# Weight tiles of octets 6 and 7 of the second head group move to the end of the stream

## The chip, the cores and the metric

One core of one Trainium2 chip. The metric is the time of one execution on the device in microseconds (us), the median of several runs. The profile shows one execution of the program, with its span from the first instruction to the last.

## The reference, cut to what matters

Attention with a feature map gives x; a spectral mix over 64 modes and a product with `w_ch` follow.

```python
def phi(x):
    proj = np.einsum('bhsd,df->bhsf', x, w_phi)
    proj = proj - np.max(np.abs(proj), axis=-1, keepdims=True)
    return np.concatenate([np.exp(proj), np.exp(-proj)], axis=-1)
q_p, k_p = phi(q), phi(k)
kv = np.einsum('bhsf,bhsd->bhfd', k_p, v)
z = np.sum(k_p, axis=2)
x = einsum('bhsf,bhfd->bhsd', q_p, kv) / (einsum('bhsf,bhf->bhs', q_p, z)[..., None] + 1e-06)
# x is put together as (8 batches, 576 rows, 512 = 8 heads x 64)
X = np.fft.rfft(x, axis=1)[:, :64]
Y[:, :64] = X @ (w_r + 1j * w_i)      # for each mode m a 512 x 512 matrix
u = x + np.fft.irfft(Y, n=576, axis=1)
out = u + np.maximum(u @ w_ch, 0.0)
```

`q`, `k`, `v` are (8, 8, 576, 64), `w_r` and `w_i` (64, 512, 512), all float32: the two weights alone are 134 MB.

## The kernel before, in words

**Tiles and units.** The 512 channels are split into four head groups g = 0 to 3 (two heads, 128 channels), the batches into four pairs bp. Attention runs over 16 units (g, bp). The 64 modes are split into eight *octets* o. A *weight tile* holds, for one group of 128 input channels and one octet, either w_r or w_i (1 MB in bfloat16, cast on the way in): 4 x 8 x 2 = 64 tiles, keys (g, 2o + i), with i = 0 for w_r and 1 for w_i. Tiles are numbered here 1 to 64 in the order of the stream. The list `wq` (lines 359 to 365) is that order: all 16 tiles of groups 0 and 1, then 12 tiles (octets 0 to 5) each of groups 2 and 3, and last octets 6 and 7 of groups 2 and 3, eight tiles. POOL issues all loads of weights, `kb`, `qb` and most of `vn` on one queue, in program order. A tile has one of nine buffers (`pw`), and each `next_w` issues the next load once its buffer is free.

**Attention loop** (lines 514 to 588, steps n = -2 to 16). Each step works on several units at different stages, then `freq` and `keep_x` bring a finished unit's spectrum to `XTb[g % 2]`: two buffers, so group g + 2 writes over group g. When a group's last unit is through (n = 4, 8, 12, 16), its keys join `mixq`. `some` takes keys from it, eight or nine in step 4, three in a later one (one more in step 12), calls `mix` (line 473: eight matmuls of the tile with the spectrum, 0.66 us in all at full clock) and issues the next load. Sums over the groups go to `yacc`.

**End phase.** After the loop come the remaining tiles in `while mixq` (line 977). `left` is the number of tiles still in `mixq` after the one just mixed. When the last tile of an octet is mixed, the octet's result y is transposed and multiplied by `w_ch` to give z (the octet step), and `park` puts both aside. Between tiles, `fill` takes pieces from the list `todo`:

- `turn` and `hold(i)`: transposes of one of 36 chunks of 128 rows of x (`xT`, copied from PSUM by DVE) and its product with `w_ch`, copied to `xw` by ACT. The inverse DFT tables (`inverse_tables`) are made by DVE and ACT in steps, one for each `hold`. The last three chunks' products stay in PSUM (`Channels.hold`) and are ended by `only_x` and `only_w`.
- `Absorb.all` for the other 33 chunks: adds the inverse transform of octets 0 to 5 (or 0 to 6) to x and to xw. It needs `lay`, which spreads the parked octets over the batches of a pair by DVE (two transposes of about 0.6 us), and so octet 5. For each chunk DVE adds to x, and ACT copies to xw; every second one of the first 28 takes another way (`aside`), where ACT copies to `rl` and POOL adds to xw. `full` is their order; chunks of the `direct` pairs, which need octet 6 as well, come last.

How many pieces go behind a tile is computed from `left` (lines 996 to 1001). Behind the last mix only what octets 6 and 7 still add remains: `Pair` and the written-out order `plan` (line 640), the relu, the sum and the stores by SP.

**Order.** All engine calls go through `InOrder` (line 29), which keeps them in program order on their engine. The profile therefore gives line 37, that of the helper, for all of them, and groups are told by their tiles' names: `pt<-wt,XT` is a mix, `pt<-ident_b,xs` a `turn`, `pt<-wchb,xT` the product of a `hold`, `pt` or `pp<-yall,CI` and `<-zall,CI` an `Absorb`.

Of the kernel before, what the change touches and what calls it, by code (L numbers as in the profile page):

```python
# [43 lines left out]
def kernel(  # L44
# [311 lines left out]
        return wt  # L356

    wts = {}
    wq = [(g, mg) for g in range(2) for mg in range(2 * NO)]
    wq += [(g, mg) for g in (2, 3) for mg in range(12)]  # L360
    wq += [(g, 2 * o + i) for o in (6, 7) for g in (2, 3) for i in range(2)]
    order = list(wq)
    wq.remove((0, 5))
    wq.insert(1, (0, 5))
# [108 lines left out]
    def mix(g, w, wt, XT, bank):  # L473

        o, i = w // 2, w % 2
        late = g >= 2 and o >= 6
        first, last = i == 0 and not (late and g == 3), i == 1 and not (late and g == 2)
        if first:
            pys[o] = bank()
        py = pys[o]  # L480
        for r in range(2):
            for j in range(4):
                pe.matmul(
                    py[32 * j:32 * j + 32, :],
                    lhsT=XT[:, i, r, :, :, :, 4 * o + j].rearrange("p t x b -> p (t x b)"),
                    rhs=wt[:, j, r, :], start=(first and r == 0), stop=(last and r == 1),
                )
        if last and g == 0:
            act.copy(yacc[:, o, :], pys.pop(o))
        elif last and g < NG - 1:  # L490
            dve.tensor_tensor(
                out=yacc[:, o, :], in0=pys.pop(o), in1=yacc[:, o, :], op=ALU.add)
# [22 lines left out]
    for n in range(-2, len(units) + 1):  # L515
        P, Q, K, R = (unit(n + i) for i in (-1, 0, 1, 2))
        X = 0 if n < 4 else 6 if n == 4 else 3
        end = n == len(units)
        if Q:
            Q.exp_q(0)  # L520
        if K:
            K.rows_k(0)
            K.exp_k(0)
        if Q:
            Q.weigh_v2()
            if n + 3 == len(units):
                unit(n + 2).load_v_parts()
            elif unit(n + 2):
                unit(n + 2).load_v()
        if P:  # L530
            P.freq()
            assert not any(key[0] == P.g - 2 for key in mixq)
            P.keep_x()
            if P.bp == NP - 1:
                mixq += [key for key in order if key[0] == P.g and (P.g < 2 or key[1] < 12)]
        if Q:
            Q.cols_q(1)
            Q.exp_q(1)
        some(1 if X else 0)
        if K:  # L540
            K.rows_k(1)
            K.exp_k(1)
        if Q:
            Q.kv()
        some(2 if n == 4 else 0)
        if K:
            K.rows_q(0)
            K.rows_k(2)
            K.rows_q(2)
            K.rows_q(1)  # L550
        if Q:
            Q.cols_q(2)
            Q.keep_kv()
            Q.exp_q(2)
        if K:
            K.exp_k(2)
            K.weigh_v()
        some(1 if X and not end else 0)
        if R:
            R.turn_k(0)  # L560
        if K:
            K.shift_q()
        if R:
            R.turn_k(1)
        if Q:
            Q.num(0)
        if K:
            K.cols_q(0)
        if R and unit(n + 4):
            unit(n + 4).load_k()  # L570
        if Q:
            Q.num(6)
        if R:
            R.turn_q(0)
            R.turn_q(1)
            if unit(n + 4):
                unit(n + 4).load_q()
        if Q:
            Q.num(12)
        some(0 if end else X - 2 + (n == 12))  # L580
        if n == -1:
            forward_table()
        if n < 3:
            next_w((2, 3, 2, 3, 2)[n + 2])
        elif n == 3:
            next_w(1)
        if n == 6:
            pool.dma_start(wchb, moe_w_ch.rearrange("(dc p) e -> p dc e", p=128))
    assert not pys
    mixq += order[-8:]  # L590
    pm_cm.__exit__(None, None, None)
    pin_cm.__exit__(None, None, None)
    ps1_cm.__exit__(None, None, None)
# [121 lines left out]
    class Channels:  # L715
# [4 lines left out]
        def turn(self):  # L720
# [2 lines left out]
            for g in range(NG):  # L723
                pe.transpose(pt[:, g, :], x[:, g, :], ident_b)
            self.xT = pb.tile([128, 4, 128], BF16, name="xT")
            dve.tensor_copy(self.xT, pt)

        def product(self):
            pf = bank()
# [2 lines left out]
                          start=(g == 0), stop=(g == 3))  # L732
            act.copy(xw[:, self.bp, self.n, :], pf)

        def hold(self, pf):
            for g in range(NG):
                pe.matmul(pf, lhsT=self.xT[:, g, :], rhs=wchb[:, g, :],
                          start=(g == 0), stop=False)

    def back(p, c, bp, table, src, r, stop=True, start=False):  # L740

        if c < 8:
            pe.matmul(p, lhsT=table[r, c % 4, :], rhs=src[r, 2 * bp + c // 4, :],
                      start=start or src is yall, stop=stop)
        else:
            for i in range(2):
                pe.matmul(p[64 * i:64 * i + 64, :], lhsT=table[r, 4, 0:64],
                          rhs=src[r, 2 * bp + i, :], start=start or src is yall, stop=stop)

    class Absorb:  # L750

        def __init__(self, bp, n):
            self.bp, self.n = bp, n
            self.early = (bp, n) in direct
            self.rows = slice(0, 128)
            self.aside = False

        def sum_p(self, p):
            self.p = p
            back(p, self.n, self.bp, CI, yall, self.rows)  # L760

        def sum_q(self, q):
            self.q = q
            if not self.aside:
                pe.matmul(q, lhsT=ident_b, rhs=xw[:, self.bp, self.n, :], start=True, stop=False)
            back(q, self.n, self.bp, CI, zall, self.rows, start=self.aside)

        def keep_x(self):
            x = chunk(self.bp, self.n)
            dve.tensor_tensor(out=x, in0=self.p.rearrange("p (g e) -> p g e", g=4),  # L770
                              in1=x, op=ALU.add)

        def keep_w(self):
            w = xw[:, self.bp, self.n, :]
            if self.aside:
                if not spare:
                    t = pb.tile([128, 2, DMODEL], F32, name="rl")
                    spare.extend((t[:, 1], t[:, 0]))
                t = spare.pop()
                act.copy(t, self.q)  # L780
                pool.tensor_tensor(out=w, in0=t, in1=w, op=ALU.add)
            else:
                act.copy(w, self.q)

        def only_x(self):
            self.sum_p(bank())
            self.keep_x()

        def only_w(self):
            back(self.q, self.n, self.bp, CI, zall, self.rows)  # L790
            self.keep_w()

        def all(self):
            if full.index(self) % 2:
                p, q = bank(), bank()
            else:
                t = banks()
                p, q = t[:, 0], t[:, 1]
            self.sum_p(p)
            self.sum_q(q)  # L800
            self.keep_x()
            self.keep_w()

    chunks = [(bp, n) for bp in range(NP) for n in range(9)]
    ch = [Channels(*c) for c in chunks]
    ab = [Absorb(*c) for c in chunks]
    K = len(ch) - 3
    full = sorted(ab[:K], key=lambda c: c.early)
    spare = []
    for c in full[0:28:2]:  # L810
        c.aside = True

    tables = inverse_tables()

    def hold(i):
        next(tables, None)
        if i + 1 < len(ch):
            ch[i + 1].turn()
        if i < K:
            ch[i].product()  # L820
            return
        if i == K:
            t = banks()
            ab[i].q, ab[i + 1].q = t[:, 0], t[:, 1]
        elif i == K + 2:
            ab[i].q = bank()
        ch[i].hold(ab[i].q)

    todo = [ch[0].turn] + [lambda i=i: hold(i) for i in range(len(ch))]
    todo += [c.only_x for c in ab[K:]] + [c.only_w for c in ab[K:]] + [c.all for c in full[:-2] + full[:-3:-1]]  # L830
    A = 3 * 3 + K

    def fill(n):
        for _ in range(n):
# [31 lines left out]
    class Pair:  # L866
# [32 lines left out]
        def sums(self, side, a):  # L899
# [4 lines left out]
                          stop=True)  # L904
            else:
                r = 64 * a + 32 * z
                back(at, n, bp, CL, yl, slice(r, r + 32), True, start)
            self.left[side] -= 1

        def keep(self, a):  # L910
# [66 lines left out]
    while mixq:  # L977
# [7 lines left out]
            until("mix")  # L985
        mix(*key, wts.pop(key), XTb[g % 2], bank)
        left = len(mixq)
        if left == 11:
            yall = pw.tile([128, B_, DMODEL], BF16, name="yall", tag="wt")
        elif left == 10:  # L990
            zall = pw.tile([128, B_, DMODEL], BF16, name="zall", tag="wt")
        else:
            next_w(1)
        if left == 6:
            yl = pw.tile([128, B_, DMODEL], BF16, name="yl", tag="wt")
        if left > 8:
            n = -(-max(len(todo) - A - 2, 0) // (left - 8))
        elif left == 8:
            n = 2
        else:  # L1000
            n = math.ceil(len(todo) / max(left - 0.6, 0.4)) if left else 0
        if g == NG - 1 and i == 1:
            end = left == 0
            py = pys.pop(o)
# [8 lines left out]
                    dve.tensor_tensor(out=yst[:, H * h:H * h + H], in0=py[:, H * h:H * h + H],  # L1013
                                      in1=(yacc[:, o] if o < 6 else late[:, o - 6])[:, H * h:H * h + H], op=ALU.add)
            put(yst, o, 0, (0, 2))
            if o < 5:
                fill(min(n, 1))
            for h in range(2):
                if end:
# [7 lines left out]
                    act.copy(yT[h], pt[h])  # L1027
            if o < 7:
                park(yst, o, 0)
            if o < 5:  # L1030
                fill(min(n - 1, 1))
            cut = (slice(0, 384), slice(384, DMODEL))
            pz, marks = [], ["z0a", "z0b", "z1"]
# [16 lines left out]
            if o < 7:  # L1050
                park(zst, o, 1)
            if o == 5:
                lay(3)
                lay(0)
            elif o == 6:
                assert all(f.__self__.early or f.__self__.bp for f in todo)
                lay(0)
            fill(max(n - 2, 0) if o < 5 else n)
        else:
            fill(n)  # L1060
    assert not todo
# [33 lines left out]
```

## Time and profile before

| | |
|---|---|
| median of 3 runs | 437.66 us (436.58 to 437.86) |
| the profiled execution | 436.92 us |
| its span | 435.1 us, mean granted clock of TensorE 0.911 |
| busy share PE, DVE, ACT, POOL | 75%, 70%, 67%, 28% |
| HBM read and written | 163.64 MB, 9.44 MB |

In the page, a slice is 435.1 / 40 = 10.88 us; each digit is the busy share in tenths. The GB/s are those of the written side, so a weight tile, which is read in float32 and written in bfloat16, counts 1 MB. In a row of a timeline stand the start, the time from the first instruction's start to the last one's end, the engine, the operation with tiles and shapes, and how many were merged. A row of windows gives, for a stretch of the span, the busy time of each engine with the number of instructions, the granted clock of TensorE (1.00 is full), the DMA share and GB/s.

### The profile page before, as it was taken

Reading aid. Unit: us, or ns where it says so; the run is one execution under the profiler, and the core shown is the slowest. Engines: PE = TensorE matmul, PEld = TensorE weight load, DVE = VectorE, ACT = ScalarE, POOL = GpSimd, SP = SyncE. Lnnn points to the kernel's source line nnn. Section 1 sums busy time; section 2 is a strip of 40 time slices with the busy share of each in tenths; the row PEclk is TensorE's granted clock in tenths of the full one; section 3 lists DMA queues with packets and bytes.
Section 4 is the critical chain, followed back from the end, with each engine's and each line's share of the span. In section 5 each row is a group of like instructions: output and inputs, shape, how many; then the busy total and the mean of one; then the engine's idle time right before and its main releaser. Section 6 shows DMA issues by size and latency. Waiting matters only on the chain.

```text
span 435.1 us, 10067 instructions
## 1 busy us (share of the span) xinstructions
PE 328.3 (75%) x4205; PEld 196.1 (45%) x4205; DVE 306.7 (70%) x608; ACT 291.5 (67%) x473; POOL 120.2 (28%) x158
## 2 busy tenths in 40 slices
PE   1567668678697686886976866946899867979993
PEld 1345546456465454554654644622345433333320
DVE  6768676765676677887678879728854445997794
ACT  3788696776977978887778779613444331656871
POOL 6232132123211212222222221221111100574790
PEclk9779897789988989997789999968999998999997
DMA  9999999999999999999999999999999999993797
GB/s 215 209 211 211 238 211 238 235 214 241 235 211 239 216 232 239 237 212 238 223 226 235 213 256 216 211 212 213 212 212 212 212 212 212 212 214 80 231 392 295
DMA packets 49879, 97.71 MB, mean 225 GB/s; under 512 B 2314, under 2 KB 11530, under 8 KB 49834
## 3 DMA queue, kind: packets, MB, share of 16 engines
q0 software_dynamic: 45136, 85.40, 100.4%
q1 hardware_dynamic: 4538, 11.60, 7.1%
q8 instruction: 33, 0.54, 0.5%
q10 hardware_dynamic: 160, 0.07, 0.1%
q14 instruction: 12, 0.10, 0.1%
HBM read 163.64 MB, written 9.44 MB: 398 GB/s over the span
## 4 chain that ended last, share of the span: by engine, by line
PE 34%; ACT 26%; DMA 17%; DVE 17%; issue 4%; POOL 1%; ACTq 0%; DVEq 0%; POOLq 0%
PE one L37 13%; ACT AQ L37 11%; ACT AB L37 9%; PE pt L37 8%; DMA wt<-in_moe_w_i_dram 8%; DMA wt<-in_moe_w_r_dram 8%; PE two L37 8%; DVE m L37 5%; PE pp L37 4%; ACT XT L37 3%; ACT qT L37 2%; DVE xs L37 2%; DVE mk L37 2%; DVE of L37 1%; DVE xw L37 1%
## 5 line engine op out<-in xcount | busy, mean ns | idle before, releaser
L37 ACT ACTIVATE AQ<-two 128x1024 bf16<-128x1024 f32 x64 | 80.4, 1345 | 2.0 <-PE two L37 1.9
L37 ACT ACTIVATE AB<-two 128x1024 bf16<-128x1024 f32 x64 | 62.8, 1054 | 3.3 <-DVE mk L37 3.1
L37 ACT CAST xw<-pt 128x512 bf16<-128x512 f32 x50 | 29.4, 588 | 44.8 <-PE pt L37 44.8
L37 DVE TENSOR_REDUCE m<-two 128x8 f32<-128x1024 f32 x32 | 39.2, 1224 | 20.1 <-PE two L37 20.0
L37 POOL DMA_DIRECT2D wt<-in_moe_w_i_dram x28 | 21.0, 750 | 88.3 <-PE one L37 33.2
L37 DVE TENSOR_REDUCE mk<-two 128x8 f32<-128x1024 f32 x32 | 38.9, 1217 | 8.8 <-PE two L37 8.8
L37 PE MATMUL pt<-wchb,xT 128*128 128x512 bf16 x136 | 38.1, 406 | 8.7 <-DVE xT L37 7.2
L37 PE MATMUL two<-w2blk,qT 128*128 128x256 bf16 x128 | 21.9, 299 | 27.0 <-ACT AQ L37 14.8
L37 DVE TENSOR_TENSOR va<-vn,ee 128x1152 bf16<-128x1152 f32 x32 | 41.9, 1354 | 0.0
L37 POOL DMA_DIRECT2D wt<-in_moe_w_r_dram x30 | 22.4, 746 | 66.4 <-PE one L37 20.3
L37 PEld LDWEIGHTS <-xs 128*128 128x128 bf16 x624 | 31.8, 103 | 13.1 <-issue 7.2
L37 ACT COPY qT<-one 128x512 bf16<-128x512 bf16 (+1 forms) x32 | 19.1, 642 | 24.7 <-PE one L37 24.5
L37 PE MATMUL two<-qT,w2blk 128*128 128x512 bf16 x64 | 27.1, 424 | 9.2 <-ACT AQ L37 9.2
L37 PEld LDWEIGHTS <-qT 128*128 128x128 bf16 x144 | 14.6, 103 | 41.8 <-issue 38.7
L37 DVE TENSOR_TENSOR xs<-one,rd 128x384 bf16<-128x384 f32 x48 | 26.7, 557 | 1.6
L37 PEld LDWEIGHTS <-AQ 128*128 128x128 bf16 x512 | 24.0, 106 | 7.7 <-issue 3.7
L37 PE MATMUL one<-kvz,AQ 128*128 128x65 bf16 x512 | 26.7, 206 | 0.9 <-ACT qT L37 0.8
L37 PE MATMUL two<-mT,minus 96*128 96x512 bf16 x64 | 27.3, 426 | 0.2 <-DVE mT L37 0.2
L37 PEld LDWEIGHTS <-XT 128*32 128x32 bf16 x512 | 14.6, 149 | 28.4 <-issue 21.1
L37 POOL DMA_DIRECT2D kb<-in_k_dram x16 | 11.4, 714 | 56.8 <-PE one L37 49.4
L37 PE MATMUL one<-wt,XT 128*32 128x512 bf16 x288 | 24.7, 430 | 2.9 <-ACT XT L37 1.5
L37 DVE RECIPROCAL rd<-one 128x6 f32<-128x6 f32 x48 | 9.4, 195 | 23.7 <-PE one L37 23.4
(150 smaller groups left out, 737.1 us busy)
## 6 DMA issues: line engine op xcount, KB each, us to landing
wt<-in_moe_w_r_dram POOLq DMA_DIRECT2D x30, 1024.0 KB, 27.7
wt<-in_moe_w_i_dram POOLq DMA_DIRECT2D x28, 1024.0 KB, 28.6
out_dram<-of SPq DMA_DIRECT2D x15, 512.0 KB, 3.9
vn<-in_v_dram POOLq DMA_DIRECT2D x13, 576.0 KB, 24.7
kb<-in_k_dram POOLq DMA_DIRECT2D x16, 288.0 KB, 19.9
qb<-in_q_dram POOLq DMA_DIRECT2D x16, 288.0 KB, 18.8
xs<-in_moe_w_i_dram POOLq DMA_DIRECT2D x2, 1024.0 KB, 23.2
out_dram<-of SPq DMA_DIRECT2D x6, 256.0 KB, 3.1
```

The source lines that it names most:

```text
L37: ins = f(*args, **kwargs)
```

## The change

The tiles of octets 6 and 7 of group 1 go to the end as well: the stream is now 16 tiles of group 0, 12 each of groups 1, 2 and 3, and at the end octet 6 of groups 1, 2, 3 and octet 7 of groups 1, 2, 3: 12 tiles behind octet 5. Since group 3 writes over group 1's spectrum, POOL copies that spectrum's last eight modes of 32 aside (`kept`, in a `kb` buffer, in step 12), and ACT copies it at the end of the loop into the place of modes 16 to 24 of `XTb[0]`, which group 2 no longer needs. The last mixes of the loop fall away where group 2 is done, so that 24 tiles are mixed in the end phase, not 22; `yall` and `zall` are allocated at 15 and 14 tiles left, not 11 and 10, and no load is issued there, as before. The three chunks that were held in PSUM are treated like the others (`Absorb.all` for 36 chunks; `aside` for every second of the first 30). The first ten `xT` copies are made by ACT. `todo` is ordered anew: turn and 30 holds, then the last six holds with two sums behind each, then 24 sums; all is done with three tiles left. `Pair`, `plan` and what follows the last mix are unchanged.

```diff
-    wq = [(g, mg) for g in range(2) for mg in range(2 * NO)]
-    wq += [(g, mg) for g in (2, 3) for mg in range(12)]
-    wq += [(g, 2 * o + i) for o in (6, 7) for g in (2, 3) for i in range(2)]
+    wq = [(g, mg) for g in range(NG) for mg in range(12 if g else 2 * NO)]
+    wq += [(g, 2 * o + i) for o in (6, 7) for g in range(1, NG) for i in range(2)]
...
-        late = g >= 2 and o >= 6
-        first, last = i == 0 and not (late and g == 3), i == 1 and not (late and g == 2)
+        late = g > 0 and o > 5
+        first, last = i == 0 and (not late or g == 1), i == 1 and (not late or g == NG - 1)
+        if late and g == 1:
+            XT, o = XTb[0], o - 2
...
-                mixq += [key for key in order if key[0] == P.g and (P.g < 2 or key[1] < 12)]
+                mixq += [key for key in order if key[0] == P.g and (P.g == 0 or key[1] < 12)]
...
-        some(1 if X else 0)
+        some(1 if X and not end else 0)
...
         if R and unit(n + 4):
             unit(n + 4).load_k()
+        elif R and n + 4 == len(units):
+            kept = pin.tile([128, 2, 9, D_], BF16, name="kb").rearrange(
+                "p b c d -> p (b c d)")[:, 0:1024].rearrange("p (f m) -> p f m", m=8)
+            assert not any(key[0] == 1 for key in mixq)
+            pool.tensor_copy(kept, XTb[1].rearrange("p u r t x b m -> p (u r t x b) m")[:, :, 24:])
...
-    assert not pys
-    mixq += order[-8:]
+    assert not pys and not any(key[0] < 3 for key in mixq)
+    mixq += order[-12:]
+    act.copy(XTb[0].rearrange("p u r t x b m -> p (u r t x b) m")[:, :, 16:24], kept)
...
-            dve.tensor_copy(self.xT, pt)
+            if chunks.index((self.bp, self.n)) < 10:
+                act.copy(self.xT, pt)
+            else:
+                dve.tensor_copy(self.xT, pt)
...
-    K = len(ch) - 3
-    full = sorted(ab[:K], key=lambda c: c.early)
+    full = sorted(ab, key=lambda c: (c.early, (1, 0, 2, 3)[c.bp]))
     spare = []
-    for c in full[0:28:2]:
-        c.aside = True
+    for i, c in enumerate(full[:30]):
+        c.aside = i % 2 == 0
...
-        if i < K:
-            ch[i].product()
-            return
...
-        ch[i].hold(ab[i].q)
-
-    todo = [ch[0].turn] + [lambda i=i: hold(i) for i in range(len(ch))]
-    todo += [c.only_x for c in ab[K:]] + [c.only_w for c in ab[K:]] + [c.all for c in full[:-2] + full[:-3:-1]]
-    A = 3 * 3 + K
+        ch[i].product()
+
+    sums = [c.all for c in full[:-2] + full[:-3:-1]]
+    todo = [ch[0].turn] + [lambda i=i: hold(i) for i in range(30)]
+    A = len(sums) + len(ch) - 30
+    for i in range(30, len(ch)):
+        todo += [lambda i=i: hold(i)] + [sums.pop(0) for _ in range(2)]
+    todo += sums
...
-        if left == 11:
+        if left == 15:
             yall = pw.tile([128, B_, DMODEL], BF16, name="yall", tag="wt")
-        elif left == 10:
+        elif left == 14:
             zall = pw.tile([128, B_, DMODEL], BF16, name="zall", tag="wt")
...
-        if left > 8:
-            n = -(-max(len(todo) - A - 2, 0) // (left - 8))
-        elif left == 8:
-            n = 2
+        if left > 12:
+            n = -(-max(len(todo) - A - 3, 0) // (left - 12))
+        elif left == 12:
+            n = len(todo) - A
         else:
-            n = math.ceil(len(todo) / max(left - 0.6, 0.4)) if left else 0
+            n = math.ceil(len(todo) / max(left - 2, 1)) if left else 0
...
-            if o < 5:
+            if o < 5 or o == 6:
                 fill(min(n, 1))
...
-                lay(3)
+                lay(1)
                 lay(0)
...
-            fill(max(n - 2, 0) if o < 5 else n)
+            fill(max(n - 2, 0) if o < 5 or o == 6 else n)
```

More of the change, by code (lines that the diff above doesn't have):

```diff
@@ L475, in mix @@
         o, i = w // 2, w % 2
-        late = g >= 2 and o >= 6
-        first, last = i == 0 and not (late and g == 3), i == 1 and not (late and g == 2)
+        late = g > 0 and o > 5
+        first, last = i == 0 and (not late or g == 1), i == 1 and (not late or g == NG - 1)
+        if late and g == 1:
+            XT, o = XTb[0], o - 2
         if first:
-            pys[o] = bank()
-        py = pys[o]
+            pys[w // 2] = bank()
+        py = pys[w // 2]
         for r in range(2):
@@ L733, in product, with back @@
             act.copy(xw[:, self.bp, self.n, :], pf)
[L735 to L740, printed above, removed]
+    def back(p, c, bp, table, src, r, start):
         if c < 8:
             pe.matmul(p, lhsT=table[r, c % 4, :], rhs=src[r, 2 * bp + c // 4, :],
-                      start=start or src is yall, stop=stop)
+                      start=start, stop=True)
         else:
@@ L747, in back @@
                 pe.matmul(p[64 * i:64 * i + 64, :], lhsT=table[r, 4, 0:64],
-                          rhs=src[r, 2 * bp + i, :], start=start or src is yall, stop=stop)
+                          rhs=src[r, 2 * bp + i, :], start=start, stop=True)
     class Absorb:
@@ L754, in __init__ @@
             self.early = (bp, n) in direct
-            self.rows = slice(0, 128)
             self.aside = False
[L758 to L791, printed above, removed]
         def all(self):
@@ L798, in all @@
                 p, q = t[:, 0], t[:, 1]
[L799 to L802, printed above, removed]
+            x, w = chunk(self.bp, self.n), xw[:, self.bp, self.n, :]
+            rows = slice(0, 128)
+            pg = p.rearrange("p (g e) -> p g e", g=4)
+            back(p, self.n, self.bp, CI, yall, rows, True)
+            if not self.aside:
+                pe.matmul(q, lhsT=ident_b, rhs=w, start=True, stop=False)
+            back(q, self.n, self.bp, CI, zall, rows, self.aside)
+            dve.tensor_tensor(out=x, in0=pg, in1=x, op=ALU.add)
+            if self.aside:
+                if not spare:
+                    t = pb.tile([128, 2, DMODEL], F32, name="rl")
+                    spare.extend((t[:, 1], t[:, 0]))
+                t = spare.pop()
+                act.copy(t, q)
+                pool.tensor_tensor(out=w, in0=t, in1=w, op=ALU.add)
+            else:
+                act.copy(w, q)
     chunks = [(bp, n) for bp in range(NP) for n in range(9)]
@@ L818, in hold @@
             ch[i + 1].turn()
-        if i < K:
-            ch[i].product()
-            return
[L822 to L826, printed above, removed]
-        ch[i].hold(ab[i].q)
-    todo = [ch[0].turn] + [lambda i=i: hold(i) for i in range(len(ch))]
-    todo += [c.only_x for c in ab[K:]] + [c.only_w for c in ab[K:]] + [c.all for c in full[:-2] + full[:-3:-1]]
-    A = 3 * 3 + K
+        ch[i].product()
[5 more added lines that the diff above has]
+    todo += sums
     def fill(n):
@@ L906, in sums @@
                 r = 64 * a + 32 * z
-                back(at, n, bp, CL, yl, slice(r, r + 32), True, start)
+                back(at, n, bp, CL, yl, slice(r, r + 32), start)
             self.left[side] -= 1
@@ L1029 @@
                 park(yst, o, 0)
-            if o < 5:
+            if o < 5 or o == 6:
                 fill(min(n - 1, 1))
```

## The prediction

> **What bounds the kernel now.** First the page's slices and queues, to see which resource is never idle:
>
> ```profile
> DMA  9999999999999999999999999999999999993797
> GB/s 215 209 211 211 238 211 238 235 214 241 235 211 239 216 232 239 237 212 238 223 226 235 213 256 216 211 212 213 212 212 212 212 212 212 212 214 80 231 392 295
> ...
> q0 software_dynamic: 45136, 85.40, 100.4%
> ```
>
> The queue of the weights (q0) never rests for 36 of 40 slices; a megabyte tile lands every 4.95 us at 212 GB/s. So the kernel is a stream of loads plus what comes behind its last tile, and the change leaves the bytes of the stream as they are. Next, when the last tile (number 64) lands, from the group of weight loads, cut to its issue:
>
> ```profile
> L37 POOL DMA_DIRECT2D wt<-in_moe_w_i_dram x1: 742/742/742, 365.8 to 365.8; - x1
> ...
> DMA to landing us min/median/max: 30.2/30.2/30.2
> ```
>
> 365.83 + 30.25 = 396.08 us (tile 63 by the same view 391.2, tile 62 385.9). Is it used at once? The timeline of PE, its mixes alone:
>
> ```profile
> 380.27 0.66 PE L37 MATMUL pt<-wt,XT 128*32 128x512 bf16 x8
> ...
> 388.71 0.66 PE L37 MATMUL pt<-wt,XT 128*32 128x512 bf16 x8
> ...
> 393.01 0.66 PE L37 MATMUL pt<-wt,XT 128*32 128x512 bf16 x8
> ...
> 397.41 0.66 PE L37 MATMUL pt<-wt,XT 128*32 128x512 bf16 x8
> ...
> 401.12 0.66 PE L37 MATMUL pt<-wt,XT 128*32 128x512 bf16 x8
> ```
>
> The last mix starts at 401.12, **5.04 us after its tile has landed**, and each of the mixes before it stands behind its tile too (63: 397.41 against 391.2). The windows say why:
>
> ```profile
> core 0: us, PE busy (x) PEld busy (x) DVE busy (x) ACT busy (x) POOL busy (x), PEclk, DMA share, GB/s
> ...
> 286.60:306.90 20.30, 12.53 (x72) 5.29 (x72) 13.40 (x62) 4.75 (x7) 3.93 (x5) 0.67 1.12 212
> 306.90:345.00 38.10, 35.30 (x296) 18.33 (x296) 21.77 (x59) 17.18 (x32) 5.94 (x8) 1.00 1.12 212
> 345.00:364.90 19.90, 13.74 (x103) 6.88 (x102) 9.41 (x23) 5.13 (x11) 1.48 (x2) 0.91 1.12 212
> 364.90:401.10 36.20, 32.73 (x194) 12.82 (x193) 29.21 (x50) 21.05 (x39) 19.06 (x19) 1.00 0.94 181
> 396.10:401.10 5.00, 5.00 (x27) 1.87 (x24) 3.36 (x6) 3.33 (x7) 1.16 (x1) 1.00 0.07 17
> 401.10:435.10 34.00, 25.55 (x153) 8.13 (x152) 23.10 (x25) 20.07 (x38) 18.62 (x17) 0.92 0.78 294
> ```
>
> From 396.10 to 401.10 the DMA share is 0.07 and PE is busy all 5.00 us: it is still working off sums (the Absorb pieces), which cannot begin before octet 5 is done, at tile 56. From 345 to 364.9, however, PE is busy 13.74 of 19.90 us: there it waits for tiles. The work is there, but at the wrong end. Behind the last mix come 34.0 us (401.1 to 435.1), the same whatever happened before.
>
> **The change, part by part.** The end of the stream: same tiles, same sizes, other order, so the last still lands near 396.1 if nothing starves the queue. Eight loads are outstanding at most (a load is issued 0.5 us after the eighth before it lands: 346.85 after 346.32), about 40 us of stream. The bounds of an error here are zero and the few us by which an issue could come later than 40 us ahead; I take zero.
>
> *POOL's copy* (128x1024 bf16), in POOL's own order behind the load issued at 240.77 and ahead of the one at 245.67. No row shows it; nearest are POOL's memset of 128x1024 (0.97 us) and its addition of 128x512 (1.16 us, two inputs): 1 to 2.3 us. POOL idled 4.15 us ahead of 245.67, which hides it. Uncovered, it would delay a load that has 35 us of stream ahead of it, or ACT's and DVE's XT writes of the next unit at 248.6, by at most those 2.3 us. I take zero.
>
> *ACT's copy back*, next to `late` (128x1024, 1.05 us): 1 us, behind the last XT write (285.2 to 286.1). ACT then idled 8.65 us until 295.64; the first xT copy would now wait for it. I take 1 us at the start, in the walk below.
>
> *Mixes that move.* In the loop the four mixes of step n=12 belong to the third head group now; the first comes right behind the XT writes of its own group. The same place in step n=8 shows PE waiting 1.48 us for XT; here 1 to 2 us of PE, and none if ACT bounds the step anyway. Against that PE has two mixes fewer (1.3 us) before 287. Sum: zero.
>
> *The three PSUM-held pieces* become ordinary: 3 more additions of xw on PE (0.22 us each at the rate of the sums), with ACT copies that take the place of those which ended the held sums: 0.7 us of PE.
>
> *xT copies 0 to 9 go from DVE to ACT.* DVE loses 10 x 0.42; ACT's nearest row is qT, 128x512 bf16 from PSUM, 0.64 us. DVE makes the tables at that time (17.25 us busy from 293.6 to 313.6, 3.7 of it nine xT copies), and PE waited 7.2 us for DVE's xT in all. ACT has room there.
>
> *Where octet 5 comes.* It hangs on tile 52 (landed 336.4) instead of 56 (356.25). Before it, 28 of the 31 pieces (turn and holds) are to be done, three or two a tile; after it, 42 pieces in ten steps down to three tiles before the end: 5, 5, 5, 5, 5, 5, 4, 4, 4 and none behind. Walk of PE, by tile:
>
> - Tile 41 now opens the end phase. XT is written by 286.8: start 287, against 291.58 for tile 43, for which PE had waited 3.87 us. Up to tile 45: 12 holds of 1.1 us (four transposes, four matmuls), 4 mixes of 0.66 and octets 0 and 1 of 1.5 (a step with an octet took 5.45 us, without 3.96): 18.8 us. The clock was 0.50 from 286.2 to 296.4, worth 5 us. yst and yT of both octets stand behind table pieces on DVE, and ACT's first copy behind 1 us: 4 us (bounds 0, and 13, the tables as a whole). Sum 28: tile 45 at 315.
> - Tiles 45 to 51 at the spacings seen from 318.67 to 338.17 for the same content: 3.96 + 5.45 + 2.87 + 4.36 + 2.87 + 4.36 + 2.87 = 26.7: tile 52 at 341.7.
> - Octet 5 with its four lays and two holds took 8.56 us, 1 of it by half clock; with three holds 8.7: tile 53 at 350.4.
> - Four steps with the six last holds and 14 sums: 6 x 1.1 + 14 x 0.6 (DVE's spacing of sums) + 4 x 0.66 = 17.6, 368.0. Five sums and a lay, 5.0 (six took 5.63): tile 58 at 373.0. Octet 6 took 8.44 with six sums, 7.8 with five: 380.8. Three steps of four sums, 3.15 each (six took 4.4): tile 62 at 390.3.
> - Tile 63 lands at 391.2; its mix and the base matmuls that took 399.31 to 401.12 (1.8) end at 393.7. **Tile 64: PE is ready 2.4 us before it lands.**
>
> So the last mix starts at 396.1, not 401.12: minus 5.0. **Next late** is the stream itself.
>
> *What the wait costs.* PE now idles ahead of the last mix, behind which the whole tail is queued. From 354.50 to 357.90 PE was busy 1.04 of 3.40 us, and the granted clock of the next 3.4 us was 0.50; after a stretch busy 1.61 of 3.40 it stayed 1.00. Idle 2.4 us may do either: 0 to 1.7 us (half of one such stretch); I take 0.8.
>
> The Trainium skill ("TensorE: Matmul & The Clock Gate", the section on the HAM clock gate) says that PE falls to half clock after at least one idle window of about 3.4 us; read strictly that needs a longer gap than 2.4 us, and by it the 0.8 would be 0. This trace speaks against the strict reading: the stretch with 1.04 us of work was not idle.
>
> **Sum**: -5.0 + 0.8 = -4.2 us. Profiled execution 436.92 (span 435.1, 1.8 around it): 432.7. The median of the runs shown is 0.74 above that execution: **433.4 us**.
>
> **Rivals.**
> 1. *PE is not ready at 396.* My walk has 2.4 us of room. Beyond it every us is lost one for one: 432.7 (no idle, no half clock) up to 437.7. For: DVE was the pace of the sums (29.2 of 36.2 us). Against: four tiles more to do it in.
> 2. *Slower: octets 0 and 1 are caught in the tables.* Their yst and yT copies are in DVE's queue between table pieces whose Sin is in ACT's queue between xT copies, and PE's products wait for both. If that costs the 13 us instead of 4, tile 45 comes at 324, and the last mix at 396.1 + 9 - 2.4 = 402.7, 1.6 late: 439. It decides from 7.4 us beyond my walk. For: PE was busy 12.53 of 20.30 us here already. Against: holds lie between, and two-tile steps catch up.
> 3. *The stream starves*: five last loads now stand between POOL's additions (1.16 us each), which wait for ACT. It needs 20 us of delay; 1 us lost would give 434.4, but 5 would give 438.
> 4. *The gain is given back in the tail*: it is the same instruction list, stores at 372 to 389 GB/s from 410 on. Two half-clock stretches: 437.66 - 5.0 + 3.4 = 436.1.
>
> **How the numbers follow.** Chances: forecast 0.62, rival 1 0.18, rival 2 0.10, rival 3 0.05, rival 4 0.05. About 0.3% (1.3 us) is what a measurement can tell from no change. Faster: 0.62 + 0.13 + 0.02 + 0.03 = 0.80; within: 0.05 + 0.02 + 0.01 + 0.01 = 0.09; slower 0.11. Range: low 437.66 - 5.0 and 1 us for my sizes, 431.6; high into rival 1, 437.0. That leaves out most of rival 2, part of 3 and the end of rival 1, under 2 in 10.
>
> **What would show it.** Right: last tile landing within 0.5 us of 396.1, last mix within 1 us behind it, PE idle ahead of it, a tail of 34 to 36 us, tile 52's mix between 336 and 346. Wrong: PE without a gap before the last mix (rival 1), tile 45's mix beyond 320 (rival 2), a gap of q0 before 390 (rival 3).

## The result, and the profile after

The changed kernel takes **431.93 us** (median of 4 runs, 431.48 to 432.76) against 437.7 (4 runs, 436.58 to 437.86): ratio 0.9876, 95% interval 0.9851 to 0.9900. The profiled execution takes 432.76, its span 430.9: 4.2 less than before (435.1), the 4.2 of the forecast's sum.

The page's slices and queue, as before the change:

```profile
DMA  9999999999999999999999999999999999997797
GB/s 211 210 211 211 238 213 237 224 225 238 240 210 233 216 237 238 238 211 239 212 239 222 226 244 229 212 212 212 212 212 213 212 211 212 212 212 161 244 395 288
...
q0 software_dynamic: 45136, 85.40, 101.3%
```

The stream has the same packets and bytes and no new gap. The slice that stood at 80 GB/s is at 161: slices are shorter now, so that this one begins at 387.8 us, not at 391.6, and holds more of the stream. The last load, from its group:

```profile
L37 POOL DMA_DIRECT2D wt<-in_moe_w_i_dram x1: 782/782/782, 369.3 to 369.3; - x1
...
DMA to landing us min/median/max: 26.4/26.4/26.4
```

It lands at 369.25 + 26.36 = 395.61, 0.47 earlier than before. (In the other profiled executions, of both kernels and their variants, it lands at 395.67 to 396.49, so this much is no proof of a faster stream.) The timeline of PE at the end (start, us, work, and in brackets the idle time ahead and what ended it):

```profile
389.12 0.66 PE L37 MATMUL pt<-wt,XT 128*32 128x512 bf16 x8
390.66 0.67 PE L37 MATMUL pt<-wt,XT 128*32 128x512 bf16 x8 [0.87 <-DMA wt<-in_moe_w_r_dram]
391.25 1.13 PE L37 MATMUL pt<-late,eye 128*128 128x512 f32 x2
392.22 0.38 PE L37 MATMUL pt<-xs,ident_b 128*128 128x512 bf16 x1
392.43 0.81 PE L37 MATMUL pp<-xw,ident_b 128*128 128x512 bf16 x3
395.65 0.84 PE L37 MATMUL pt<-wt,XT 128*32 128x512 bf16 x8 [2.41 <-DMA wt<-in_moe_w_i_dram]
```

The last mix begins 0.04 us behind its tile, not 5.04, and PE waits 2.41 us for it. The windows, with two stretches around that wait:

```profile
core 0: us, PE busy (x) PEld busy (x) DVE busy (x) ACT busy (x) POOL busy (x), PEclk, DMA share, GB/s
286.60:306.90 20.30, 14.16 (x106) 6.64 (x104) 17.15 (x72) 14.14 (x25) 3.15 (x4) 0.93 1.12 212
306.90:345.00 38.10, 34.27 (x286) 18.07 (x288) 21.05 (x53) 16.35 (x32) 5.19 (x7) 1.00 1.12 212
345.00:364.90 19.90, 17.57 (x115) 7.59 (x117) 10.80 (x21) 9.73 (x18) 7.88 (x8) 1.00 1.12 212
364.90:395.70 30.80, 24.43 (x150) 9.09 (x152) 20.75 (x37) 15.14 (x29) 15.17 (x17) 1.00 1.08 209
395.70:430.90 35.20, 26.73 (x150) 8.55 (x151) 23.06 (x25) 20.08 (x38) 18.61 (x17) 0.89 0.76 287
...
392.60:396.00 3.40, 0.99 (x11) 0.45 (x9) 0.00 (x0) 0.00 (x0) 0.00 (x0) 1.00 0.77 181
396.00:399.40 3.40, 3.39 (x19) 1.27 (x12) 1.01 (x3) 1.05 (x3) 0.68 (x1) 0.50 0.26 65
```

From 345 to 364.9 PE is busy 17.57 us, where it was 13.74: the work has moved into the waits. The stretch before the last mix has 0.99 us of work in 3.40, and the next runs at clock 0.50. So the tail takes 35.2 us, not 34.0. The last mix stands 5.00 us less behind its tile, the tile lands 0.47 sooner, and 1.22 are given back: 4.25, the difference of the spans.

### The profile page after: what moved, and what is told of

It reads as the page before. It is cut to its first block, busy times and chain, and to the rows that moved or that the text cites. A ratio compares the mean times of both kernels' runs of the same rounds, so it can differ in the third digit from the quotient of the medians.

```text
span 430.9 us, 10044 instructions
## 1 busy us (share of the span) xinstructions
PE 324.9 (75%) x4162; PEld 195.6 (45%) x4207; DVE 302.7 (70%) x596; ACT 299.1 (69%) x487; POOL 122.2 (28%) x160
## 4 chain that ended last, share of the span: by engine, by line
PE 34%; ACT 24%; DMA 20%; DVE 14%; issue 4%; POOL 2%; ACTq 0%; POOLq 0%; DVEq 0%
DMA wt<-in_moe_w_i_dram 14%; PE pt L37 13%; PE one L37 11%; ACT AQ L37 10%; ACT AB L37 7%; PE two L37 6%; DMA kb<-in_k_dram 6%; DVE m L37 5%; PE pp L37 3%; ACT qT L37 3%; ACT XT L37 2%; DVE xs L37 2%; DVE xw L37 2%; DVE of L37 1%; DVE mk L37 1%
## 5 line engine op out<-in xcount | busy, mean ns | idle before, releaser
L37 ACT CAST xw<-pt 128x512 bf16<-128x512 f32 x54 | 31.8, 588 | 26.9 <-PE pt L37 26.7
L37 PE MATMUL pt<-wchb,xT 128*128 128x512 bf16 x135 | 37.0, 387 | 8.9 <-DVE xT L37 2.4
L37 PE MATMUL two<-w2blk,qT 128*128 128x256 bf16 x128 | 23.9, 319 | 24.1 <-ACT AQ L37 13.6
L37 PE MATMUL one<-wt,XT 128*32 128x512 bf16 x272 | 23.8, 438 | 3.4 <-ACT XT L37 3.4
L37 PE MATMUL two<-w2blk,kT 128*128 128x256 bf16 x128 | 21.1, 293 | 5.1 <-ACT AB L37 5.1
L37 PE MATMUL one<-CF,xs 128*128 128x64 bf16 (+2 forms) x480 | 23.2, 204 | 1.8 <-DVE xs L37 1.2
## 6 DMA issues: line engine op xcount, KB each, us to landing
kb<-in_k_dram POOLq DMA_DIRECT2D x16, 288.0 KB, 19.6
```

What stands on the lines that cost most here:

```text
L37: ins = f(*args, **kwargs)
```

## The experiments

Two theories. **Stream**: the last mix was late because the sums could open only at tile 56; opened at tile 52, they end before tile 64 lands, and the stream's end is the floor. **Pieces**: the gain comes from what was made cheaper on the way (xT copies on ACT, no pieces held in PSUM). Where a ratio is given, it is to the kernel before, timed beside it (there 436.3 to 436.5 us).

**One part alone: xT copies on ACT, in the kernel before** (before_act).

```diff
-            dve.tensor_copy(self.xT, pt)
+            if chunks.index((self.bp, self.n)) < 10:
+                act.copy(self.xT, pt)
+            else:
+                dve.tensor_copy(self.xT, pt)
```

> The kernel before with the first ten xT copies on ACT, nothing else of the change. Theory: PE comes earlier to tile 55 and waits there for the tile; octet 5 still hangs on tile 56 at 356.25, and what follows is as before: 437.7 within 0.7. Rival (cheaper pieces made the gain): 434 to 436.

Measured 437.14 us, ratio 1.0013 (0.9997 to 1.0029). PE's mixes of tiles 56, 57 and 64 in its timeline:

```profile
355.77 0.66 PE L37 MATMUL pt<-wt,XT 128*32 128x512 bf16 x8 [1.40 <-DMA wt<-in_moe_w_i_dram]
363.69 1.08 PE L37 MATMUL pt<-wt,XT 128*32 128x512 bf16 x8
...
401.31 0.66 PE L37 MATMUL pt<-wt,XT 128*32 128x512 bf16 x8
```

PE comes sooner, waits for tile 56, and the last mix is as late as ever. So ACT's copies alone bring nothing. The other part of the pieces theory, no pieces held in PSUM, was not run by itself; the run late10 below has both parts and still loses part of the gain.

**That part undone in the changed kernel** (xt_dve): the edit above, the other way round.

> The changed kernel with all xT copies on DVE again, as before. Theory (the gain comes from tile 52 instead of 56 opening the sums): DVE has 4.2 us more between 287 and 315, where it is busy 17.15 of 20.30 us, so tile 45 comes up to 4 us later; PE has 0.87 + 2.41 us of waiting behind that, so the last mix is 0 to 1 us behind its tile: 431.0 to 433. Rival (the gain comes from cheaper pieces, this one above all): most of it is gone, 435 to 437.

432.86 us, ratio 0.9909 (0.9880 to 0.9939). From tile 41 to tile 45 PE took 29.6 us, against 26.1 in the changed kernel. The copies cost at most these 3.5 us, as half clock lasted 6.8 us there, not 3.4. The last mix still stands 0.04 behind its tile, with 2.27 us of waiting left, since this execution's loop ended 2.2 us sooner. Most of the gain stays.

**Less work behind octet 5, weights in the old order** (before_drop10, before_drop20).

```diff
-    ... + [c.all for c in full[:-2] + full[:-3:-1]]
-    A = 3 * 3 + K
+    ... + [c.all for c in (full[:-2] + full[:-3:-1])[10:]]      # or [20:]
+    A = 3 * 3 + K - 10                                          # or 20
```

> The kernel before with ten of its 33 Absorb pieces left out (their part of the inverse transform is missing in the output): 6 us of DVE's and PE's work behind octet 5 are gone, the order of the weights is as before. Theory (all of the gain is the 5.04 us that the last mix stands behind its tile): PE is ready at 395, the last mix follows tile 64 at once, 5.0 us less, and up to 1.2 back by half clock: 432.7 to 433.9. Rival (cheaper pieces or another order of the stream made the gain): the full 6 us less, or nothing.

> The kernel before with 20 of 33 Absorb pieces left out: 12 us of work gone. Theory: the stream's end is the floor, so no more than with ten: 5.0 less and 1.2 back by half clock, 433.9. Rival (work bounds the end throughout): 12 us less, 426.

432.32 us, ratio 0.9901 (0.9885 to 0.9916), and 430.94, 0.9871 (0.9856 to 0.9887). The last mixes, first with ten and then with 20 left out:

```profile
396.53 0.66 PE L37 MATMUL pt<-wt,XT 128*32 128x512 bf16 x8 [1.40 <-DMA wt<-in_moe_w_i_dram]
```

```profile
396.36 0.66 PE L37 MATMUL pt<-wt,XT 128*32 128x512 bf16 x8 [1.98 <-DMA wt<-in_moe_w_i_dram]
```

Ten pieces less bring the last mix to its tile, ten more leave it there: the floor is the stream. Neither paid half clock in the tail. The times came out lower than expected for another reason too: the expectations start from 437.7 us, and the kernel before took 436.46 beside these runs. With 20 the tail was 32.9 us, 1.1 shorter than with ten; its first store is issued at the same distance from the last mix (5.15 us), its last one lands 1.0 sooner after that mix. Why is open.

**Ten tiles behind octet 5, not twelve** (late10): octet 6 of the second group stays in the loop.

```diff
-    wq = [(g, mg) for g in range(NG) for mg in range(12 if g else 2 * NO)]
-    wq += [(g, 2 * o + i) for o in (6, 7) for g in range(1, NG) for i in range(2)]
+    wq = [(g, mg) for g in range(NG) for mg in range((16, 14, 12, 12)[g])]
+    wq += [(g, 2 * o + i) for o in (6, 7) for g in range(8 - o, NG) for i in range(2)]
...
-        if left > 12:
-            n = -(-max(len(todo) - A - 3, 0) // (left - 12))
+        if left > 10:
+            n = -(-max(len(todo) - A - 3, 0) // (left - 10))
```

> The changed kernel with ten tiles behind octet 5, not twelve: octet 6 of the second head group stays where it was, octet 7 moves. The tables' stage begins with tile 43, which lands 4.9 us after 41. Theory (what counts is when octet 5 can open the sums): PE waits for tile 54 (345.9), and reaches tile 64 about 7 us later than with twelve, less two mixes: 2 to 3 us after its landing, without the idle gap and so at full clock: span 432 to 433, between both kernels (435.1 and 430.9). Rival (the rest of the change makes the gain): 430.9, as with twelve.

433.89 us, ratio 0.9929 (0.9901 to 0.9957); span 433.6. Tile 54's mix and part of the last one:

```profile
346.18 0.66 PE L37 MATMUL pt<-wt,XT 128*32 128x512 bf16 x8 [1.99 <-DMA wt<-in_moe_w_i_dram]
...
399.93 0.45 PE L37 MATMUL pt<-wt,XT 128*32 128x512 bf16 x4
```

PE waits 2 us for the tile that opens the sums, and the last mix is 4.0 us behind tile 64 (395.92): a place between 5.04 and 0.04, though a us later than I had worked out. The estimate had left out two stretches at half clock behind that wait (347.08 to 350.49 and 353.91 to 357.32), and the profiled execution, 435.38 us, is the slowest of seven; the median's span, 432.0, is the low end of what was expected. Where the sums open sets the time.

**The copies left out** (no_copies): `kept`, POOL's and ACT's copy are gone.

> The changed kernel without the two copies that keep group 1's spectrum (POOL and ACT); the mixes of its late tiles read group 2's spectrum instead, so this part of the result is left out. Theory: both copies are hidden, 431.9 within 0.7. Rival (the wait of ACT's copies or POOL's loads behind them costs): 1 to 2 us less.

432.32 us, ratio 0.9895 (0.9863 to 0.9927): no gain that can be told. In the changed kernel POOL's copy takes 1.05 us at 242.03, with 3.11 us of idle time behind it. ACT's copy is not hidden where it stands. The first three rows are the changed kernel, the last one is no_copies:

```profile
285.84 1.04 ACT L37 COPY XT<-kb 128x1024 bf16<-128x1024 bf16 x1
287.87 1.07 ACT L37 COPY xT<-pt 128x512 bf16<-128x512 bf16 x2
288.76 0.81 PE L37 MATMUL pt<-wchb,xT 128*128 128x512 bf16 x3 [1.54 <-issue]
```

```profile
291.88 0.81 PE L37 MATMUL pt<-wchb,xT 128*128 128x512 bf16 x3 [0.68 <-ACT xT L37]
```

PE idles 1.54 us ahead of the first product with the copy, 0.68 without it. So the copy costs PE 0.9 us there, and the room ahead of tiles 63 and 64 hides it.

**Is the wait real room, and what does the half clock cost?** Matmuls into a bank that nobody reads, ahead of the last mix: ten, 24, and five each ahead of tiles 63 and 64 (busy10, busy24, busy5_5).

```diff
+            idle = bank()
+            for _ in range(10):
+                pe.matmul(idle, lhsT=ident_b, rhs=wchb[:, 0, :], start=True, stop=True)
         mix(*key, wts.pop(key), XTb[g % 2], bank)
```

> The changed kernel with ten matmuls (128x512) put ahead of the last mix, into a PSUM bank that nobody reads: 2.2 us of work for PE in the 2.41 us in which it waits for tile 64. Theory (the last mix waits for the stream, and the idle gap ahead of it brings half clock for 3.4 us): the last mix still starts 0 to 0.2 us behind its tile, the granted clock stays 1.00 from 392 on, the tail goes from 35.25 us back to 34.0: 1.0 to 1.3 us less than the changed kernel in its profile, about 430.9 in its time (431.93 there). Rival (PE is still late at 396, and the gap is only how the profile shows it): ten matmuls come on top, 434.

> The same with 24 matmuls, 5.2 us. Theory: 2.4 us are hidden, 2.8 are not; the last mix starts 2.8 us behind its tile, the clock stays full (1.2 back): 431.93 + 2.8 - 1.2 = 433.5, 2.6 us more than with ten. Rival: 5.2 on top, 437.

> The changed kernel with five unread matmuls (1.1 us) ahead of the mix of tile 63 and five ahead of that of tile 64. With ten ahead of tile 64 the half clock came earlier, from 392.29, after the wait for tile 63 (1.9 us there), and stretched the ten themselves. Theory (half clock follows a stretch in which PE works less than about half the time): with the work spread over both waits neither stretch is that empty; PE is ready for tile 64 at 394.6 or before, its mix follows the landing, the clock stays 1.00, the tail takes 33.8 to 34.0 instead of 35.2: span 429.6, where the loop ends about as in the changed kernel (its tile 41 at 286), 1.3 below it. Where the loop ends 3 us later (it did in two runs), the last mix is 1.3 late, span 430.9. Rival (half clock is not set by these waits): span 431 to 432 again.

busy10: 433.25 us, ratio 0.9911 (0.9884 to 0.9938), span 431.5. Not what was expected, and its windows tell why:

```profile
388.90:392.30 3.40, 1.47 (x17) 0.70 (x15) 0.65 (x1) 0.58 (x1) 0.00 (x0) 1.00 1.09 216
392.30:395.70 3.40, 3.40 (x8) 0.98 (x7) 0.00 (x0) 0.00 (x0) 0.00 (x0) 0.50 0.78 187
```

The wait for tile 63 (1.93 us here) had already emptied a stretch, so half clock came while the ten matmuls ran, and the last mix was 1.7 us behind its tile. The tail, at full clock, took 33.8. busy24 met the same from 390.40: 435.56 us, ratio 0.9981 (0.9955 to 1.0006), last mix 4.2 us behind its tile, not 2.8. So the price of work past the room is seen, but the room of 2.4 us is not measured cleanly by these two.

busy5_5: in the profile as expected, last mix at 395.79 (tile at 395.75), no half clock from 307 to 426, tail 33.9, span 429.7, 1.2 below the changed kernel. But this was the fastest of six executions; their median is 432.47, ratio 0.9907 (0.9872 to 0.9941). The likely cause is that in others the loop ends later and PE has no such room, as busy10_base shows next; no trace shows it for this kernel.

**A base matmul moved ahead of the last mix as well** (busy10_base, `db021` ahead of `mix` in `plan`).

> The changed kernel with ten matmuls ahead of the last mix as in the first run, and with the base matmul of pair 02's second half, which stands behind the last mix, moved ahead of them. Theory: as with ten matmuls, and 0.2 us less behind the last mix: 430.7, the fastest of all. Rival: the move costs or gives nothing, 430.9.

433.68 us, ratio 0.9933 (0.9914 to 0.9952). Here the loop ended late (tile 41 mixed at 288.89, not 286.00), the ten matmuls came on top, and the last mix was 2.1 us behind its tile. The theory's time failed: in this execution the room was not there.

**The changed kernel again, and its sums spread evenly** (changed_again, even_end).

```diff
-            n = math.ceil(len(todo) / max(left - 2, 1)) if left else 0
+            n = math.ceil(len(todo) / max(left - 0.6, 0.4)) if left else 0
-        "eb000 db020 db000 db001 mix db021 ...
+        "eb000 db020 db000 db001 db021 mix ...
```

> The changed kernel once more, beside the others of this call, since the loop's end differed from execution to execution by 7 us at one and the same instruction order (tile 41 mixed at 282.8 to 290.0). Theory: last mix 0 to 1 us behind tile 64, ratio to the kernel before 0.988 within 0.004. Rival (one lucky draw): ratio above 0.993.

> The changed kernel with its sums spread to the last tile but one (the old formula, left - 0.6 for left - 2, gives 5, 4, 4, 4, 4, 4, 4, 4, 4, 4, 1 pieces), and with the base matmul of pair 02's second half moved ahead of the last mix. No work is added: the two waits of PE, ahead of tiles 63 and 64, become more alike. Theory (the stream sets the last mix; half clock hangs on how empty a stretch of 3.4 us is): the last mix follows tile 64 as before, neither stretch is under 40% busy, the tail is 33.8 to 34.0 in every execution: span 429.6 to 430.2, and the median 0.5 us or so below that of the changed kernel (ratio 0.986). Rival (the pace of the sums counts): PE comes later to tile 64, and the ratio is above 0.989.

changed_again: 431.48 us, ratio 0.9873 (0.9846 to 0.9900), last mix 0.04 us behind its tile, after 2.21 us of waiting. Yet no half clock: its stretches of 3.4 us lie otherwise against the wait. Where they lie is read from the half clock elsewhere in the same trace: here it begins at 285.91 and at 425.86, 41 stretches of 3.413 us apart.

```profile
391.70:395.10 3.40, 2.29 (x14) 0.82 (x7) 0.00 (x0) 0.00 (x0) 0.00 (x0) 1.00 0.83 187
395.10:398.50 3.40, 1.98 (x17) 0.88 (x16) 0.90 (x3) 0.67 (x2) 0.00 (x0) 1.00 0.21 55
```

Its tail took 34.05 us. The three profiled executions with half clock right behind the last mix (changed kernel, xt_dve, no_copies) have tails of 34.97 to 35.20, the others, before_drop20 aside, 33.63 to 34.05: it costs 0.9 to 1.6 us.

even_end: 431.83 us, ratio 0.9909 (0.9883 to 0.9936). That is on the rival's side of 0.989, and not told apart from the changed kernel; the gain of 0.5 us did not show, though in its profile the last mix kept to its tile with the loop ending 2.9 us later, and the tail took 33.9 (span 429.9). No variant that does all the work was shown to beat the changed kernel.

## Why the prediction was right, point by point

- **What bounds the kernel, and the -5.0**: right. The last mix went from 5.04 us behind its tile to 0.04; leaving work out reached the same floor in the old order; with ten tiles it was 4.0 behind.
- **The walk**: tile 41 at 286.0 (287 forecast), 45 at 312.1 (315), 52 at 338.8 (341.7), 53 at 347.6 (350.4), 58 at 370.8 (373.0), 62 at 389.1 (390.3); waiting ahead of tile 64 2.41 (2.4). From 41 to 62 it took 103.1 us (103.3), but that is luck in part, as its terms were off both ways. The first stage took 26.1, not 28: half clock cost 1.7 us there (3.4 us at 0.50, from 303.86), not 5, and PE waited 6 us (2.4 for xT from ACT, 2.1 for yst and yT, 1.5 for which the profile names no cause, 0.9 of it ACT's copy by no_copies, 0.2 for xw), not 4. Tiles 53 to 57 took 19.6 (17.6), 57 to 59 9.7 (12.8), 59 to 62 12.2 (9.5). Nor do the 2.41 us test the walk: PE already waited 0.87 for tile 63, so they are the 5.0 us between the landings of tiles 63 and 64, less the work between.
- **The wait's price, 0.8**: between 0 and 1.7 as bounded. The profiled execution paid 1.2, changed_again nothing. What others paid has no trace, but six of the ten executions of the changed kernel have spans of 429.5 to 429.7, as a landing at 395.6 and a tail of 34.0 give without half clock. By the strict reading of the clock rule of the Trainium skill ("TensorE: Matmul & The Clock Gate", section on the HAM clock gate), under which a whole window of about 3.4 us must be idle, it would be 0 every time; the stretch that was busy 0.99 of 3.40 us contradicts that reading. The same section of the Trainium skill also calls the window free-running, and here the traces agree: 2.41 and 2.21 us of the same wait gave half clock in one execution and full in another.
- **POOL's copy and starving at zero**: right (3.11 us of idle time behind the copy, and no gap in q0). **ACT's copy back, 1 us in the walk**: 0.9 by no_copies.
- **The median**: 433.4 was forecast, 431.93 measured, 0.3 above the low end of the range. I put the median 0.74 above the profiled execution, as before the change; it lay 0.83 below. That offset was the mis-sized term. The sum of the mechanism, 4.2, was right to 0.1, with luck: the tile landed 0.47 sooner (taken as zero), and the wait cost 1.2, not 0.8. Against the 437.7 of the kernel before the gain is 5.8; beside changed_again that kernel took 436.51, and the gain is 5.0.
- **The rivals**: rival 1 did not decide here, but its room is thin, as busy10_base shows. Rivals 2 and 3 did not come, and of rival 4's two half-clock stretches behind the last mix one did, the one in the sum.

## What to carry to other kernels

When a stream of loads is the floor, look at how long after its last landing the last user starts, and for waits on the same engine earlier: order the loads so that what opens the other work comes sooner, and work moves from the end into the waits. Check with a run that leaves work out whether the floor is where you think. Padding a wait with unread work was no gain here: the room changes from execution to execution, and the work stays when the room is gone.

## What the runs showed of the hardware

Half clock does not need an idle stretch, and no sharp border of busy time was found. In stretches of 3.4 us, 0.99, 1.22 (busy24) and 1.47 us of PE work were followed by 0.50, and 1.61 (before), 1.78 (before_drop20) and 2.29 by 1.00. But no_copies, after a wait of only 1.27 us for tile 64, shows 1.81 us followed by 0.50:

```profile
394.83:398.24 3.41, 1.81 (x16) 0.85 (x16) 0.72 (x2) 0.37 (x1) 0.00 (x0) 1.00 0.34 96
398.24:401.65 3.41, 3.19 (x15) 1.60 (x14) 0.58 (x2) 1.94 (x4) 1.43 (x2) 0.50 0.30 77
```

Elsewhere 1.54 us (busy5_5, from 341.39) were followed by 1.00 and 2.02 (changed_again, from 282.50) by 0.50. So between 45% and 59% busy either happened; what else decides is open.

The end of the attention loop moved from execution to execution: tile 41's mix, up to which the instruction order is the same, began at 283.8 (xt_dve) to 288.9 us (even_end, busy10_base). (The 290.0 in the expectation of changed_again is no_copies, which lacks the two copies; 282.8 fits only before_drop20, with the old loop.) Executions whose half clock fell alike ended the loop alike: in the changed kernel and busy5_5 it began at 269.72 and 269.71, and tile 41 at 286.00 and 285.85; in even_end and busy10_base at 273.73 and 273.91, and tile 41 at 288.86 and 288.89. So how the clock's stretches lie against the program is a likely cause; no run varies that alone.
